# A long convolution on TensorE: reading the moving operand from the loaded kv tile instead of from a built copy

## The chip, the core and the metric

The kernel runs on one NeuronCore of a Trainium2 chip. The time is device microseconds from start to end of one execution; smaller is better. The kernel before takes 864.24 us, the median of three runs (859.52 to 866.49). The profile is of another execution of the same kernel, which took 879.67 us, with a span of 877.8 us from the first to the last instruction.

## The reference

Two independent layers on sequences of S = 2048 with D = 640 channels, all in bf16. Their outputs lie side by side.

```python
# A: a gated long convolution (H3)
k_shift = sum over t < 4 of k[s - t] * shift_k[:, t]
kv = k_shift * v
y = causal convolution of kv with ssm_k along the sequence, per channel (2048 taps)
a = q * (y + kv * ssm_D)
# B: full softmax attention, 32 heads of 20
q, k, v = x @ wqkv
b = softmax(q k^T * 20 ** -0.5) v @ wo
out = concatenate([a, b])
```

The convolution is written as an FFT in the reference; the kernel computes it directly, with matmuls. `ssm_D` is added to the first tap.

## The kernel before

**Attention.** Queries come in four chunks of 512, heads in eight groups of four, keys in 16 blocks of 128. A score unit is one head, one key block, one query chunk: 128 x 512 numbers in one PSUM bank. `S_task` (L629) computes two or three units, then `EXP_task` (L671) has ScalarE take the exponential of two or three banks at once and write bf16 probabilities into slots of `P_sb`. There are 2048 units. When ScalarE would be late, a unit goes to VectorE: `chain_start` reads the bank (L691), and for two units together `chain_end` works out the exponential in six steps (L726 to L731, then L721 or L723). `PV_task` (L749) multiplies four probability tiles with V. The rest (projections L473, transposes L447 and L773, output L835) is fitted between.

**Convolution.** A prologue on VectorE (L558) computes kv and stores it in a DRAM scratch, each block of 32 positions reversed. For each channel the stationary operand is a window of the kernel's taps (`HK`, a Toeplitz matrix loaded with overlapping rows), and the moving operand holds the channel's kv values, 16 blocks of time as 16 columns, in two parities. `conv_task` (L964) does 16 channels: per channel eight matmuls (L982), each with 26 to 32 columns, adding into one PSUM bank. 40 tasks, 5120 matmuls. Three VectorE steps fold the bank into `Y`; `A_iter` multiplies by q.

The moving operand is built. `kvr_load` brings 80 channels of kv into `KVr` as [128, 64 steps, 80 channels]: the values of one channel at successive steps lie 80 elements apart. `kvx_build` has GpSimd copy them (L957) into `KVX`, two tiles of 16 channels in turn, so that a channel's columns lie side by side. Each build is two copies of 512 elements. There is one `KVr` tile: after the fifth build it is loaded again.

**Order of work.** It is decided when the program is built. `Prog` keeps an estimated time per engine (`T`), and a main loop puts the next score group on PE when its bank is expected free, else whatever fits the slack: side tasks by due time (`pend`), convolution matmuls one by one (each taken as `CQ` = 0.026 us), `PV_task`, or matmuls on zeros (`fill`, L376) when PE streams too little. `dve_run` orders VectorE by priorities, `pool_run` GpSimd's copies. VectorE steps marked `two` are put off while a GpSimd copy is thought to run (`pbusy`). `want_vec` gives a unit to VectorE if its backlog is below `VQ`. All DMA loads of the convolution go through SyncE's queue, in the planned order. So any change of a cost or a buffer reorders the whole program.

**SBUF.** One region `R` holds, in turn, the prologue's tiles and then the convolution's tiles plus `NPX` extra probability slots. `NPU` slots exist in all.

```python
dst = sub(KVX[i], [[64, 8], [16, 4], [1, 16]], 512 * z)                  # kvx_build: operand, side by side
src = sub(KVr, [[1, 8], [80, 4], [320, 16]], t % 5 * 16 + 8 * z)         # from steps of 320 elements
rhs = sub(KVX[i], [[32, 2], [1, n]], (4 * u + x) * 64 + r1 * 16)         # conv_task: moving operand
```

## Time and profile before

| | busy us, or count |
|---|---|
| span | 877.8 |
| PE matmul (ends modelled) | 849.1 |
| ScalarE | 826.4 |
| VectorE | 772.5 |
| GpSimd | 103.0, of which copies L957 90.8 |
| convolution matmuls L982 | 5120, 178 ns each (modelled, overlapping) |
| zero matmuls L376 | 435 |

Busy times overlap between engines and don't add up to the span. [...]the distance between starts, best seen at the weight loads (PEld), says more about the rate. The mean granted TensorE clock in this execution is 0.949 of full speed.

### The profile page before, as it was taken

Reading aid. Unit: us, or ns where it says so; the run is one execution under the profiler, and the core shown is the slowest. Engines: PE = TensorE matmul, PEld = TensorE weight load, DVE = VectorE, ACT = ScalarE, POOL = GpSimd, SP = SyncE. Lnnn points to the kernel's source line nnn. Section 1 sums busy time; section 2 is a strip of 40 time slices with the busy share of each in tenths; the row PEclk is TensorE's granted clock in tenths of the full one; section 3 lists DMA queues with packets and bytes.
Section 4 is the critical chain, followed back from the end, with each engine's and each line's share of the span. In section 5 each row is a group of like instructions: output and inputs, shape, how many; then the busy total and the mean of one; then the engine's idle time right before and its main releaser. Section 6 shows DMA issues by size and latency. Waiting matters only on the chain.

```text
span 877.8 us, 27035 instructions
## 1 busy us (share of the span) xinstructions
PE 849.1 (97%) x11659; PEld 359.4 (41%) x11659; DVE 772.5 (88%) x1582; ACT 826.4 (94%) x738; POOL 103.0 (12%) x95
## 2 busy tenths in 40 slices
PE   9999999998999999999999999999999999999998
PEld 5432332222345444444344444435444443443432
DVE  4457899998699999999999999999998999986794
ACT  6799999998799999999999999999998999997796
POOL 3000000003021111121112001211120211010000
PEclk9999999999599999999999999999998999985599
DMA  9614422228259887878866867897595789584512
GB/s 282 220 37 141 140 91 91 91 62 140 67 140 185 177 189 164 176 170 184 175 150 164 171 165 186 201 173 170 145 182 113 185 188 187 142 188 110 115 26 59
DMA packets 172994, 130.35 MB, mean 148 GB/s; under 512 B 76977, under 2 KB 170155, under 8 KB 172875
## 3 DMA queue, kind: packets, MB, share of 16 engines
q1 hardware_dynamic: 170683, 125.51, 61.9%
q0 software_dynamic: 736, 2.75, 0.9%
q8 instruction: 92, 1.51, 0.8%
q10 hardware_dynamic: 1456, 0.37, 0.2%
q14 instruction: 27, 0.22, 0.1%
HBM read 120.58 MB, written 10.61 MB: 149 GB/s over the span
## 4 chain that ended last, share of the span: by engine, by line
DVE 34%; PE 34%; ACT 30%; issue 1%; DVEq 0%
ACT R L671 30%; PE PS L629 10%; PE PS L982 7%; DVE XV L691 7%; PE PS L749 5%; PE PS L376 4%; DVE XF L728 4%; DVE XF L731 3%; PE PS L473 3%; DVE R L721 3%; DVE R L558 3%; DVE XF L729 2%; DVE XF L726 2%; DVE XF L727 2%; PE PS L835 1%
## 5 line engine op out<-in xcount | busy, mean ns | idle before, releaser
L671 ACT ACTIVATE R<-PS 128x1024 bf16<-128x1024 f32 (+1 forms) x730 | 821.8, 1353 | 37.8 <-PE PS L629 37.2
L629 PE MATMUL PS<-QT,KT 20*128 20x512 bf16 x2048 | 294.7, 400 | 13.6 <-ACT R L671 5.3
L982 PE MATMUL PS<-R 128*128 128x32 bf16 (+3 forms) x5120 | 216.2, 178 | 0.2
L982 PEld LDWEIGHTS PS<-R 128*128 128x128 bf16 x5120 | 165.5, 97 | 109.4 <-issue 101.4
L691 DVE TENSOR_SCALAR XV<-PS 128x512 uint16<-128x512 f32 x249 | 170.5, 687 | 32.1 <-PE PS L629 30.3
L749 PE MATMUL PS<-R,V_sb 128*21 128x512 bf16 x2048 | 172.4, 400 | 3.2 <-DVE R L721 2.3
L629 PEld LDWEIGHTS PS<-QT,KT 20*128 20x128 bf16 x2048 | 71.4, 91 | 209.2 <-ACT R L671 155.4
L957 POOL COPY R<-R 128x512 bf16<-128x512 bf16 x80 | 90.8, 1135 | 519.0 <-PE PS L982 474.2
L376 PE MATMUL PS<-Zt 128*128 128x512 bf16 x435 | 144.9, 404 | 1.2 <-DVE Zt L370 1.0
L731 DVE TENSOR_TENSOR XF<-XF 128x1024 bf16<-128x1024 bf16 x125 | 88.8, 711 | 0.9
L728 DVE TENSOR_TENSOR XF<-XF 128x1024 bf16<-128x1024 bf16 x125 | 87.6, 704 | 0.4
L749 PEld LDWEIGHTS PS<-R,V_sb 128*21 128x21 bf16 x2048 | 37.5, 90 | 75.1 <-issue 46.2
L558 DVE TENSOR_TENSOR R<-R 128x640 bf16<-128x640 bf16 x128 | 61.2, 487 | 2.5
L721 DVE TENSOR_TENSOR R<-XF,XV 128x1024 uint16<-128x1024 bf16 x81 | 58.2, 719 | 0.8
L473 PE MATMUL PS<-xT,WQ 128*20 128x512 bf16 (+1 forms) x660 | 52.8, 396 | 3.6 <-DVE XV L691 3.6
L729 DVE TENSOR_SCALAR XF<-XF 128x1024 bf16<-128x1024 uint16 x125 | 54.2, 436 | 0.6
L726 DVE TENSOR_SCALAR XF<-XV 128x1024 uint16<-128x1024 uint16 x125 | 53.2, 435 | 0.1
L727 DVE TENSOR_SCALAR XF<-XF 128x1024 bf16<-128x1024 uint16 x125 | 52.5, 427 | 0.3
L376 PEld LDWEIGHTS PS<-Zt 128*128 128x128 bf16 x435 | 35.2, 99 | 38.1 <-issue 28.1
L473 PE MATMUL PS<-xT,R 128*20 128x512 bf16 (+2 forms) x660 | 45.5, 374 | 0.3 <-DVE QT L459 0.2
L723 DVE TENSOR_TENSOR R<-XF,XV 128x512 uint16<-128x512 bf16 x87 | 34.6, 425 | 0.4
L459 DVE CAST KT<-PS 128x512 bf16<-128x512 f32 (+1 forms) x32 | 21.4, 675 | 14.6 <-PE PS L473 14.5
(56 smaller groups left out, 347.9 us busy)
## 6 DMA issues: line engine op xcount, KB each, us to landing
R<-kext_scratch SPq DMA_DIRECT2D x640, 136.0 KB, 3.4
R<-in_A_k_dram SPq DMA_DIRECT2D x15, 640.0 KB, 4.0
kext_scratch<-in_A_ssm_k_dram POOLq DMA_DIRECT2D x1, 2560.0 KB, 11.5
R<-in_A_v_dram SPq DMA_DIRECT2D x16, 160.0 KB, 5.8
kvr_scratch<-R SPq DMA_DIRECT2D x16, 160.0 KB
R<-kvr_scratch SPq DMA_DIRECT2D x8, 320.0 KB, 5.8
R<-in_A_q_dram SPq DMA_DIRECT2D x64, 40.0 KB, 3.1
out_dram<-R SPq DMA_DIRECT2D x64, 40.0 KB, 3.1
```

Of the source, the lines that this page charges most:

```text
L376: P.op("pe", lambda e: e.matmul(bank[bk], Zt, zrhs, start=start, stop=start, skip_group_check=True), reads=[b_Zt], writes=[bkb[bk]], tok=s ...
L473: ins = e.matmul(bank[bk][32 * i:32 * i + DH, 0:n], Wt[:, cc, off + i * DH:off + (i + 1) * DH], xT[:, cc, x0:x0 + n], start=(cc == 0), sto ...
L558: P.op("dve", lambda e: e.tensor_tensor(o, a, b, op), reads=reads, writes=writes, c=0.486, two=True)
L629: ins = e.matmul(bank[b0 + i], KT[32 * u:32 * u + DH, g, kb * 128:(kb + 1) * 128], QT[32 * u:32 * u + DH, qs(qc, g), :], start=True, stop= ...
L671: P.op("act", lambda e: e.activation(P_sb[:, s0:s0 + m, :], PS[:, b0 * 512:(b0 + m) * 512].rearrange("p (u q) -> p u q", u=m), ACT.Exp, sc ...
L691: work(0.2, [(lambda e: e.tensor_scalar(V, bank[bk], scale * 1.4426950408889634 * 128.0, 127.0 * 128.0, op0=ALU.mult, op1=ALU.add), [bkb[b ...
L721: last = [(lambda e: e.tensor_tensor(o, Q2, V2, ALU.add), bv + [bq], [b_P[z] for z in zs], two, True)]
L728: (lambda e: e.tensor_tensor(Q, Q, F.bitcast(U16), ALU.mult), [bf, bq], [bq], two, True),
L731: (lambda e: e.tensor_tensor(Q, Q, F, ALU.mult), [bf, bq], [bq], two, True)] + last, end)
L749: ins = e.matmul(bank[OBANK][32 * u:32 * u + DH + 1, :], V_sb[:, kb, 4 * g + u, :], P_sb[:, slot[4 * b + u], :], start=first, stop=last, t ...
L957: steps.append((lambda e, dst=dst, src=src: e.tensor_copy(dst, src), [cv["KVr"]], [kx], 1.3, False))
L982: P.op("pe", lambda e, o=o, lhsT=lhsT, rhs=rhs, st=st, k=k: e.matmul(o, lhsT, rhs, start=st, stop=k == 7, skip_group_check=True), reads=rd ...
```

## The change

The moving operand is read where the load put it. `KVr` now holds 64 channels, and a channel's successive columns lie 4 x 64 elements, 512 bytes, apart; the matmul's access pattern steps over them. `kvx_build`, `KVX`, `pool_run` and GpSimd's part in the convolution go. There are two `KVr` tiles in turn (ten loads instead of eight), and the next load of a tile goes out when the last of its four convolution tasks is planned. The purpose is to save GpSimd's copies, [...]and a link in the chain from load to matmul. The two larger tiles need room: probability slots go from 35 to 33. Several of the planner's constants change with it.

```diff
-NPU, NPX = 35, 11
+CHW, NKR = 64, 2
+NPU, NPX = 33, 9
-OBS = 99
+OBS = 28
-KBV, KBW, LONE = 13, 12, 16
+KBV, KBW, LONE = 13, 12, 24
-KV0, KVPACE, APACE, VQ, CONVE, ZTH, AGE, WAIT3 = 25.0, 0.8, 0.25, 4.5, 60, 2.3, 32, 0.4
+KV0, KVPACE, APACE, VQ, CONVE, ZTH, AGE, WAIT3 = 20.0, 0.8, 0.25, 4.5, 70, 2.4, 40, 0.4
-ZSL, ZLO = 0.45, 1.8
+ZSL, ZLO = 0.3, 1.8
...
-        KVr = carve(KVR_E).rearrange("p (j c) -> p j c", j=64)
-        KVX = [carve(KVX_E) for _ in range(2)]
+        KVr = [carve(KVR_E).rearrange("p (j c) -> p j c", j=64) for _ in range(NKR)]
...
         def kvr_load(b):
-            P.dmas("sp", [(KVr[32 * a:32 * a + 32, 16 * a:64, :],
-                           ap(kvr_d, [[D, 32], [32 * D, 64 - 16 * a], [1, 80]], 80 * b)) for a in range(4)],
-                   d_kvr, reads=b_kvd, writes=[cv["KVr"]], slow=2)
+            P.dmas("sp", [(KVr[b % NKR][32 * a:32 * a + 32, 16 * a:64, :],
+                           ap(kvr_d, [[D, 32], [32 * D, 64 - 16 * a], [1, CHW]], CHW * b)) for a in range(4)],
+                   d_kvr[b % NKR], reads=b_kvd, writes=[cv["KVr"][b % NKR]], slow=2)
...
-        def kvx_build(t):
-            i = t % 2
-            kx = cv["KVX"][i]
-            steps = []
-            for z in range(2):
-                dst = sub(KVX[i], [[64, 8], [16, 4], [1, 16]], 512 * z)
-                src = sub(KVr, [[1, 8], [80, 4], [320, 16]], t % 5 * 16 + 8 * z)
-                steps.append((lambda e, dst=dst, src=src: e.tensor_copy(dst, src), [cv["KVr"]], [kx], 1.3, False))
-            pworks.append(Work(0, steps, lambda: kvr_load(t // 5 + 1) if t % 5 == 4 and t < 39 else None))
...
-                        rhs = sub(KVX[i], [[32, 2], [1, n]], (4 * u + x) * 64 + r1 * 16)
+                        rhs = sub(KVr[i], [[2 * CHW, 2], [4 * CHW, n]], r1 * CHW + c0 + 4 * u + x)
...
-                            if u == 3 and bt + 2 < 40:
-                                kvx_build(bt + 2)
+                            b = bt * 16 // CHW
+                            if u == 3 and c0 + 16 == CHW and b + NKR < D // CHW:
+                                kvr_load(b + NKR)
```

## The prediction

> **What bounds the kernel now.** I read the page's totals first, then the groups, the waits, the span in stretches of 5 us with the chain beside them, and the timeline around the odd stretches.

> ```profile
> PE 849.1 (97%) x11659; PEld 359.4 (41%) x11659; DVE 772.5 (88%) x1582; ACT 826.4 (94%) x738; POOL 103.0 (12%) x95
> ...
> PEclk9999999999599999999999999999998999985599
> ...
> L671 ACT ACTIVATE R<-PS 128x1024 bf16<-128x1024 f32 (+1 forms) x730 | 821.8, 1353 | 37.8 <-PE PS L629 37.2
> L982 PE MATMUL PS<-R 128*128 128x32 bf16 (+3 forms) x5120 | 216.2, 178 | 0.2
> L957 POOL COPY R<-R 128x512 bf16<-128x512 bf16 x80 | 90.8, 1135 | 519.0 <-PE PS L982 474.2
> ```

> PE's 97% is modelled ends, so I don't take PE for the bound. ScalarE is: one line, the exponential, is busy 821.8 us of a span of 877.8, and loses only 37.2 us to late score matmuls. The waits say the same from the other side:

> ```profile
> PEld PS L629 <- ACT R L671: 155.4, 384, 1.6
> ...
> ACT R L671 <- PE PS L629: 37.2, 59, 4.1
> ```

> The score matmuls wait 155.4 us for ScalarE to hand back PSUM banks. PE also runs 435 matmuls on zeros that compute nothing. So PE has slack on average, and VectorE (88%) has some too.

> Where do the 37.2 us lie? In the stretches of 5 us, columns are PE, PEld, DVE, ACT, POOL busy, then the granted clock:

> ```profile
> 210.00:215.00 5.00, 3.74 (x38) 0.86 (x36) 4.97 (x7) 4.27 (x5) 4.80 (x4) 1.00 0.74 139
> 215.00:220.00 5.00, 3.90 (x28) 0.68 (x27) 3.44 (x7) 2.85 (x4) 0.02 (x1) 0.58 0.00 0
> 220.00:225.00 5.00, 5.00 (x31) 0.75 (x29) 2.60 (x6) 3.44 (x4) 0.00 (x0) 0.50 0.00 0
> ```

> The clock falls to half in three stretches: 215 to 245, about 660 to 667, and 782 to 839 us. ScalarE is busy 21.3 of 30 us in the first, 11.3 of 15 around the second (655 to 670), and 45.4 of 60 around the third: lost are 8.7, 3.7 and 14.6 us, together 27.0. The profiled execution took 879.7 us; without these it would be 852.7. The timed median, 864.2, lies 11.5 above that, near the first two together (12.4). I take it that these two recur and the third mostly doesn't; that is an inference.

> What starts the first is in the timeline:

> ```profile
> 210.01 5.01 POOL L957 COPY R<-R 128x512 bf16<-128x512 bf16 x4 [10.27 <-DMA R<-kvr_scratch]
> 210.37 1.32 DVE L726 TENSOR_SCALAR XF<-XV 128x1024 uint16<-128x1024 uint16 x1
> 211.73 1.22 DVE L727 TENSOR_SCALAR XF<-XF 128x1024 bf16<-128x1024 uint16 x1
> 212.87 0.68 DVE L691 TENSOR_SCALAR XV<-PS 128x512 uint16<-128x512 f32 x1
> 213.69 0.39 PE L629 MATMUL PS<-QT,KT 20*128 20x512 bf16 x3 [1.14 <-DVE XV L691]
> 214.13 2.06 ACT L671 ACTIVATE R<-PS 128x1024 bf16<-128x1024 f32 x2 [0.73 <-PE PS L629]
> ```

> Four operand copies run back to back on GpSimd. Two VectorE steps that take 422 ns at the median take 1320 and 1220. The PSUM read behind them is not slower, but starts late, so its bank comes free late, PE idles 1.14 us, ScalarE 0.73, and half clock follows. At 655.49 two copies (2.78 us) stretch the same kind of step to 1.31 us and PE's next weight loads wait 0.67 and 0.92 us for that same PSUM read; half clock follows there too.

> [...]422 becomes 1320, while the PSUM reader stays at 680. [...]half clock follows PE's idling. [...]34 convolution weight loads take 0.92 us, last one 0.096, so (0.92 - 0.096)/33 = 25.0 ns. [...]

> **The change, part by part.**

> *Copies removed.* 80 copies of 1135 ns, 90.8 us of GpSimd, which is idle otherwise. GpSimd itself is on no path. What they cost VectorE: mean over median times count, over the seven SBUF steps of the vector exponential: 124 x (14 + 7 + 19 + 15 + 27 ns) + 81 x 32 + 87 x 6 = 10.2 + 2.6 + 0.5 = 13.3 us. That is small because the planner puts other work beside a copy, and VectorE has about 105 us idle. On the path it counts where it set off half clock: up to 8.7 + 3.7 us. I credit the first in full, since the four queued copies are the setup of the convolution, and half of the second[...]: -8.7 - 1.8 = -10.5.

> *The plan's new split.* The build shows 260 units on VectorE against 249, and exponentials 412 of 1024 and 321 of 1536 columns with 3 of 512, against 391, 339 and 2. Back to back, two of 1536 take 2.79 us with 1.45 for the last: a step of 1.34; three of 1024 take 2.86 with 1.02: 0.92. So ScalarE gets 21 x 0.92 - 18 x 1.34 + 0.5 = -4.3 us, on the path. VectorE gets 11 units: per pair of units two reads at 0.60, three scalar steps at 0.34 and three tensor steps at 0.60 (starts in its timeline) make 4.0 us, so 2.0 each, 22 us. Hidden: 13.3 regained and 105 idle stand against it.

> *The moving operand.* Each matmul now reads 26 to 32 columns of bf16, each 512 bytes from the last. Lower bound: nothing, if reading stays under the 25 ns. Nearest rows for strided reads: VectorE reads PSUM with 64 bytes between elements at full rate (256 elements 418 ns, 512 contiguous 687: the same slope with one overhead). GpSimd's copy, stepping 640 bytes in SBUF, needs 1097/512 = 2.14 ns an element; 29 columns at that rate are 62 ns, my upper bound. [...]The contiguous rate is 512 columns in about 216 ns (eight V-product matmuls, four at a time, end 0.21 us after four), 0.42 ns each; doubled 0.84, so 32, 30, 28, 26 columns take 26.9, 25.2, 23.5, 21.8 ns. Only the first two exceed 25: 1280 x (1.9 + 0.2) = 2.7 us over all. I take this value. Most hides in PE's wait for ScalarE. To see how much, I summed for each gap between score groups in the new order PE's work at the steps above against 0.45 us of ScalarE per score unit: 44 gaps overrun by 6.5 us at 24.8 ns, 59 by 9.3 at 27.5. A fifth of that difference: +0.5. The same sum gives +7 at 30 ns, +30 at 40, +60 at 50, +106 at 62.

> *Loads.* Ten of 640 KB instead of eight of 800: the same 6.4 MB, but 51,200 rows of 128 bytes for 40,960 of 160. A part lands in 4.6 to 6.8 us; with two tiles a load goes out when its tile's last convolution is done, four tasks ahead of need. Convolution runs from 226 to 842 us in 40 tasks, 15.4 us each, so 60 us of lead hide it. The new wait is the transfer queue's, for that last matmul; behind it stand weight loads that wait for the same matmul already. GpSimd's clearing grows from 3.3 to two of 2.6 us (by elements); only the first holds the first load. Nothing on the path.

> *Fewer probability slots (33 for 35), 446 zero matmuls for 435, other constants.* 11 x 0.216 = 2.4 us of PE in gaps; 17 more stand ahead of the convolution, where the first half-clock stretch was. Counted zero.

> Sum: 864.2 - 10.5 - 4.3 + 0.5 = 849.9, say **850 us**.

> **Rivals.** *Strided reads slow TensorE* (chance 0.16). [...]Against: the 25 ns floor leaves room for a halved rate, and PE waits 155 us for ScalarE. At 40 to 62 ns the overruns give 850 + 30 to 850 + 106: 880 to 956, more if stalled columns also lower the clock. *The gain is eaten* (0.22): half clock comes from thin stretches of small matmuls, as at 782 us, where no stretched VectorE step stands ahead, and the new order has its own; or the step becomes 30 ns (+7); or VectorE's extra 22 us holds banks. Then 864.2 - 4.3 and a few us either way: 856 to 868. The main case has 0.62, 840 to 856: a little above 840 if all 27 us of half clock were gone too, as 852.7 - 4.3 = 848 is the floor of the order of before, less some of the smaller VectorE delays.

> The range, 838 to 872, takes in the first two cases and leaves out most of the slow one. Faster by over 1% means under 855.6, slower over 872.9.

> **What would show it.** No GpSimd copies and no VectorE SBUF step over about 0.8 us; the exponential's busy time near 817 us; no half clock near 215 us; convolution weight loads still 25 to 26 ns apart within a run. Wrong if that distance is 30 ns or more, or if ScalarE's waits for the score matmuls exceed 37 us at full clock.

## The result, and the profile after

The changed kernel takes 1199.6 us against 865.4, medians of four executions each: the ratio is 1.386, 95% interval 1.372 to 1.399. Executions of one kernel differ in how long the clock stays at half (the kernel before took from 850.0 us at a mean clock of 1.000 to 881.6 at 0.944), so the ratios, and the times from the table on, are of executions within 1.5% of the fastest of that kernel on the same occasion. Forecast were 850 us, with a range to 872. The rival "strided reads slow TensorE" had given 880 to 956; the result is beyond that too.

The page of the changed kernel: totals, the granted clock in 40 slices, the exponential (L672 now), convolution weight loads and matmuls (L972), and the zero matmuls.

```profile
PE 1182.2 (99%) x11656; PEld 500.5 (42%) x11670; DVE 790.0 (66%) x1616; ACT 866.3 (72%) x742; POOL 14.4 (1%) x16
...
PEclk9999997565568665577655569555875555655659
...
L672 ACT ACTIVATE R<-PS 128x1024 bf16<-128x1024 f32 (+1 forms) x734 | 861.8, 1253 | 316.7 <-PE PS L630 313.0
...
L972 PEld LDWEIGHTS PS<-R 128*128 128x128 bf16 x5120 | 288.3, 119 | 172.1 <-issue 169.3
L972 PE MATMUL PS<-R 128*128 128x32 bf16 (+3 forms) x5120 | 357.4, 228 | 0.2 <-DVE R L993 0.2
...
L376 PE MATMUL PS<-Zt 128*128 128x512 bf16 x446 | 199.5, 524 | 1.0 <-DVE Zt L370 1.0
```

The zero matmuls of the kernel before:

```profile
L376 PE MATMUL PS<-Zt 128*128 128x512 bf16 x435 | 144.9, 404 | 1.2 <-DVE Zt L370 1.0
```

Three things stand here. ScalarE went from 94% to 72% and now waits 313.0 us for score matmuls, against 37.2: the bound has moved to PE. A convolution matmul takes 228 ns instead of 178. And work that the change doesn't touch is slower: a zero matmul takes 524 ns instead of 404. The clock line says why. From about 195 us to the end the clock is mostly at half; the mean is 0.677 of full speed.

How far apart the convolution matmuls start is read in the timeline, from weight loads that follow each other. First the kernel before, then the changed one in a stretch at full clock (PEld alone):

```profile
300.65 0.92 PEld L982 LDWEIGHTS PS<-R 128*128 128x128 bf16 x34 [0.23 <-issue]
...
306.66 0.94 PEld L972 LDWEIGHTS PS<-R 128*128 128x128 bf16 x18 [0.23 <-issue]
307.70 0.10 PEld L630 LDWEIGHTS PS<-QT,KT 20*128 20x128 bf16 x3
308.02 0.95 PEld L972 LDWEIGHTS PS<-R 128*128 128x128 bf16 x18 [0.23 <-issue]
```

Before it is (0.92 - 0.1)/33 = 25 ns, after (0.95 - 0.1)/17 = 50 ns; the 0.1 us is the last load itself (94 ns at the shortest in the changed kernel). Over all runs of 16 or more such loads the median is 50.5 ns after and 24.7 before, and at half clock it is about the same (from one start to the next after a matmul of 28 columns: 50 ns at full and at half clock in the changed kernel, 25 and 27 before). So two questions stand: what makes the matmul take 26 ns more, and how 5120 x 25.8 ns = 132 us become 335.

### The profile page after: what moved, and what is told of

It is laid out like the page before. It is cut to its first block, busy times and chain, and to the rows that moved or that the text cites. A ratio compares the mean times of both kernels' runs of the same rounds, so it can differ in the third digit from the quotient of the medians.

```text
span 1197.3 us, 26976 instructions
## 1 busy us (share of the span) xinstructions
PE 1182.2 (99%) x11656; PEld 500.5 (42%) x11670; DVE 790.0 (66%) x1616; ACT 866.3 (72%) x742; POOL 14.4 (1%) x16
## 4 chain that ended last, share of the span: by engine, by line
PE 83%; ACT 9%; DVE 7%; issue 1%; DVEq 0%
PE PS L972 25%; PE PS L630 23%; PE PS L750 15%; PE PS L376 12%; ACT R L672 9%; PE PS L473 4%; PE PS L836 2%; DVE R L559 2%; DVE XV L692 1%; PE PS L774 1%; DVE KT L459 1%; PE PS L805 1%; DVE XF L732 0%; PE PS L531 0%; DVE XF L727 0%
## 5 line engine op out<-in xcount | busy, mean ns | idle before, releaser
L672 ACT ACTIVATE R<-PS 128x1024 bf16<-128x1024 f32 (+1 forms) x734 | 861.8, 1253 | 316.7 <-PE PS L630 313.0
L630 PE MATMUL PS<-QT,KT 20*128 20x512 bf16 x2048 | 374.2, 507 | 6.3 <-ACT R L672 1.5
L972 PEld LDWEIGHTS PS<-R 128*128 128x128 bf16 x5120 | 288.3, 119 | 172.1 <-issue 169.3
L972 PE MATMUL PS<-R 128*128 128x32 bf16 (+3 forms) x5120 | 357.4, 228 | 0.2 <-DVE R L993 0.2
L750 PE MATMUL PS<-R,V_sb 128*21 128x512 bf16 x2048 | 230.2, 523 | 2.5 <-DVE OT_sb L760 2.2
L376 PE MATMUL PS<-Zt 128*128 128x512 bf16 x446 | 199.5, 524 | 1.0 <-DVE Zt L370 1.0
L473 PE MATMUL PS<-xT,WQ 128*20 128x512 bf16 (+1 forms) x660 | 64.5, 476 | 0.0
L727 DVE TENSOR_SCALAR XF<-XV 128x1024 uint16<-128x1024 uint16 x130 | 55.5, 435 | 0.0
L990 DVE COPY ZS<-PS 64x256 f32<-64x256 f32 x40 | 16.7, 418 | 33.7 <-PE PS L972 33.3
L760 DVE CAST OT_sb<-PS 128x512 bf16<-128x512 f32 x32 | 22.0, 688 | 25.2 <-PE PS L750 25.0
L459 DVE CAST QT<-PS 128x512 bf16<-128x512 f32 (+1 forms) x32 | 21.7, 679 | 22.9 <-PE PS L473 22.9
## 6 DMA issues: line engine op xcount, KB each, us to landing
kext_scratch<-in_A_ssm_k_dram POOLq DMA_DIRECT2D x1, 2560.0 KB, 11.3
```

What stands on the lines that cost most here:

```text
L376: P.op("pe", lambda e: e.matmul(bank[bk], Zt, zrhs, start=start, stop=start, skip_group_check=True), reads=[b_Zt], writes=[bkb[bk]], tok=s ...
L473: ins = e.matmul(bank[bk][32 * i:32 * i + DH, 0:n], Wt[:, cc, off + i * DH:off + (i + 1) * DH], xT[:, cc, x0:x0 + n], start=(cc == 0), sto ...
L630: ins = e.matmul(bank[b0 + i], KT[32 * u:32 * u + DH, g, kb * 128:(kb + 1) * 128], QT[32 * u:32 * u + DH, qs(qc, g), :], start=True, stop= ...
L672: P.op("act", lambda e: e.activation(P_sb[:, s0:s0 + m, :], PS[:, b0 * 512:(b0 + m) * 512].rearrange("p (u q) -> p u q", u=m), ACT.Exp, sc ...
L727: (lambda e: e.tensor_scalar(F.bitcast(U16), V, 127, None, op0=ALU.bitwise_and), bv, [bf], one, True),
L750: ins = e.matmul(bank[OBANK][32 * u:32 * u + DH + 1, :], V_sb[:, kb, 4 * g + u, :], P_sb[:, slot[4 * b + u], :], start=first, stop=last, t ...
```

## Experiments

In each, "distance" is the median distance of convolution weight loads in runs of 16 or more: (length of the run - 0.1 us)/(count - 1). Half clock is 2 x (1 - mean clock) x span.

| run | moving operand | distance, ns | us | mean clock | half clock, us |
|---|---|---|---|---|---|
| before | built, 2 bytes apart | 24.7 | 864.2 | 0.949 | 90 |
| after | kv tile, 512 bytes apart | 50.5 | 1199.1 | 0.677 | 773 |
| e1 | built, 128 bytes | 51.2 | 1213.4 | 0.659 | 827 |
| e4 | built, 16 bytes | 52.9 | 1227.7 | 0.644 | 878 |
| e3 | built, 8 bytes | 27.9 | 868.3 | 0.970 | 52 |
| e8, e10 | built, 4 bytes | 24.7 | 843.4, 843.8 | 1.000 | 0 |
| e2 | changed plan, 2 bytes | 24.7 | 854.0 | 0.978 | 38 |
| e5 | changed plan, 114 columns side by side | 49.5 | 967.8 | 0.993 | 14 |
| e6 | changed plan, half of the channels 512 bytes | 37.6 | 980.7 | 0.870 | 253 |

Times are medians. Distance, clock and half clock are of the profiled executions, which took 879.7 us for before, 873.9 for e3 and 1235.6 for e4. In the three series of experiments the kernel before ran beside them on the same chip, with medians of 859.5, 860.1 and 859.8 us.

### e1, e4, e3: the step alone

These are the kernel before, with its plan, its copies and its loads. Only the order of elements within `KVX` changes, and with it the step between a channel's columns.

```diff
-dst = sub(KVX[i], [[64, 8], [16, 4], [1, 16]], 512 * z)
+dst = sub(KVX[i], [[1, 8], [16, 4], [64, 16]], 8 * z)      # e1
...
-rhs = sub(KVX[i], [[32, 2], [1, n]], (4 * u + x) * 64 + r1 * 16)
+rhs = sub(KVX[i], [[32, 2], [64, n]], 4 * u + x + r1 * 16)      # e1: 128 bytes
+rhs = sub(KVX[i], [[256, 2], [8, n]], (4 * u + x) // 8 * 512 + (4 * u + x) % 8 + r1 * 128)   # e4: 16 bytes
+rhs = sub(KVX[i], [[128, 2], [4, n]], (4 * u + x) // 4 * 256 + (4 * u + x) % 4 + r1 * 64)    # e3: 8 bytes
```

The last three lines are the three variants. In e4 and e3 the copies write in groups of 8 and 4 channels accordingly (not shown).

Theory L in what follows: once neighbouring columns lie too far apart, each costs TensorE about 1.67 ns, however far. The 1.67 is from the changed kernel, 57 ns after a matmul of 32 columns and 47 after one of 26. The first figures for e3 are for the case that 8 bytes are near enough.

> The kernel before, its plan unchanged, with the built operand laid out so that a channel's columns lie 128 bytes apart. Theory L[...]: convolution weight loads 48 to 50 ns apart as in the changed kernel, long stretches at half clock, and a time of 1130 to 1230 us. Theory B (the step of 512 bytes is the trouble[...]): 25 to 35 ns apart and under 950 us. Theory P (the new plan or the loads are the trouble, not the reading): time as before, 860 to 880 us.

> The same in groups of 8 channels: columns 16 bytes apart[...]. Theory L: as with 128 bytes, 48 to 50 ns and 1130 to 1230 us. If the cost grows with the step: between 25 and 48 ns, and between.

> The kernel before with the built operand in groups of 4 channels: columns 8 bytes apart[...]. [...]weight loads 25 to 27 ns apart and 855 to 880 us. If any step beyond one element costs: over 30 ns, and over 900 us.

Measured: e1 1213.4 us (ratio 1.415, 1.400 to 1.430) and e4 1227.7 (1.432, 1.412 to 1.451). Nothing of the new plan is in them, and the whole loss is. e3 takes 868.3 (862.7 and 873.9; two further executions, with more half clock, took 888.7 and 915.0; ratio 1.013, 0.999 to 1.026), which can't be told from before. Weight loads of e4 and of e3 at full clock, (1.70 - 0.1)/30 = 53 ns and (0.57 - 0.1)/17 = 28 ns:

```profile
330.32 1.70 PEld L982 LDWEIGHTS PS<-R 128*128 128x128 bf16 x31 [0.23 <-issue]
...
312.96 0.57 PEld L982 LDWEIGHTS PS<-R 128*128 128x128 bf16 x18 [0.23 <-issue]
```

Theory P (plan, loads) and theory B (something about 512 bytes) fall. The cost sets in between 8 and 16 bytes and stays the same up to 512: 52.9, 51.2, 50.5 ns. No step between 8 and 16 bytes was run, and what sets the cost in there is not shown. The page of e4 shows the clock under the plan of before:

```profile
PEclk9999999555755555657555555665555555656679
```

In e1 and e4 GpSimd's copies, which now write with a step, also grew, to 2551 and 2568 ns (1418 in e3, 1135 before), and their times hold what that costs. It may be why e4 is some 28 us slower than the changed kernel, which has no copies. The step without copies is in e2.

### e2: the changed plan without the step

```diff
-rhs = sub(KVr[i], [[2 * CHW, 2], [4 * CHW, n]], r1 * CHW + c0 + 4 * u + x)
+rhs = sub(KVr[i], [[2 * CHW, 2], [1, n]], r1 * CHW + c0)
```

> The changed kernel, its plan unchanged, with each matmul reading its columns side by side (the wrong columns of the kv tile: the convolution's numbers are not the reference's). Theories L and B: 25 ns between weight loads, the clock near full, and the time that was predicted for the change without the reading: 845 to 862 us. Theory P: still over 1100 us.

Measured: 854.0 us (853.3 and 854.7; two further executions, with more half clock, took 873.9 and 891.7), before on the same chip 859.5 (850.0 to 861.2): no difference that can be told. So the step alone makes the loss, and the rest of the change gains nothing that can be told from the noise; 850 was predicted for this part. Its profile, of the execution of 854.7 us, has VectorE undisturbed but for one step, and half clock in two places: the clock line, then the first place in stretches of 5 us (PE, PEld, DVE, ACT, POOL busy, the clock, the DMA engines' share and GB/s):

```profile
PEclk9999999999999999999999999999999589799999
...
660.00:665.00 5.00, 4.15 (x41) 1.30 (x37) 4.45 (x10) 5.00 (x5) 0.00 (x0) 0.74 0.52 137
665.00:670.00 5.00, 5.00 (x57) 1.96 (x55) 3.25 (x6) 3.33 (x4) 0.00 (x0) 0.50 0.38 81
```

No copy runs there: the new order has thin stretches of its own, as the rival "the gain is eaten" had it.

### e5, e6: the longer matmul against the slower clock

e5 makes the matmul as long as the strided one, but with data: 114 columns side by side. All go to the same PSUM columns, so the convolution's numbers are lost. e6 reads every second channel at 512 bytes.

```diff
 # e5
-rhs = sub(KVr[i], [[2 * CHW, 2], [4 * CHW, n]], r1 * CHW + c0 + 4 * u + x)
-o = sub(bank[MISC], [[256, 2], [1, n]], (4 * u + x) * 16 + d)
+rhs = sub(KVr[i], [[2 * CHW, 2], [1, 57]], r1 * CHW + c0)
+o = sub(bank[MISC], [[256, 2], [1, 57]])
 # e6
+rhs = sub(KVr[i], [[2 * CHW, 2], [4 * CHW if x % 2 else 1, n]], r1 * CHW + c0 + (4 * u + x) * (x % 2))
```

> The changed kernel, its plan unchanged, each convolution matmul reading 114 columns side by side instead of 26 to 32 at 512 bytes (wrong columns, all added into the same ones: the convolution is left out in effect). The matmul takes as long as the strided one, but the array streams all the while. Theory C (waiting for the operand keeps the array idle, the clock is gated to half, and that is most of the loss): weight loads about 50 ns apart, the clock above 0.95, and 880 to 950 us. Theory D (the 26 ns more per matmul are the loss by themselves): about 1200 us.

> The changed kernel, its plan unchanged, every second channel read at 512 bytes, the others side by side (wrong columns for these). Mean distance about 38 ns, 66 us more of matmul than with none strided. If the loss is in proportion: about 1030 us. [...]with the clock mostly full 880 to 920 us, with it mostly half over 1080 us.

The page of e5:

```profile
PE 951.8 (99%) x11656; PEld 478.2 (49%) x11670; DVE 784.4 (81%) x1616; ACT 844.9 (87%) x742; POOL 14.4 (1%) x16
...
PEclk9999999979999999999999999999999999999999
```

and its matmuls, kept apart by shape:

```profile
L972 PE MATMUL PS<-R 128*128 128x114 bf16 x5120 | 355.1, 215 | 0.2 <-DVE R L993 0.2
...
L376 PE MATMUL PS<-Zt 128*128 128x512 bf16 x446 | 144.4, 391 | 1.0 <-DVE Zt L370 1.0
```

The same order of instructions, the same 50 ns, and 967.8 us instead of 1199.1: the clock stays at 0.993, the zero matmul takes 391 ns. (It is 18 us above the range expected.) So of some 345 us between e2 and the changed kernel, 968 - 854 = 114 come from the longer matmul and 1199 - 968 = 231 from the clock. e6, with 38 ns, is at 980.7 and 0.870. In proportion it would be 854 + 345/2 = 1027. It lies between the two sides that were written down, so it says only that the loss grows faster than the share of strided matmuls.

Over all twelve traces, from 20 us to the last windows, each of the 42 full-clock windows filled under 0.40 was followed by half clock, 40 of the 94 between 0.40 and 0.50, and none above 0.52; no window under 0.74 brought full clock back. So filling under about half puts the clock at risk, and only filling of about three quarters or more brought it back, and that not each time. This is an estimate, worked out from starts and shapes. What the runs show is that the time a strided matmul takes beyond 0.42 ns a column, in which I take its columns to stall, works like idle time, while PE shows 99% busy: e5 and the changed kernel have the same order and the same distance (49.5 and 50.5 ns), and differ in how much of it columns stream and in the clock (0.993 and 0.677).

### e7, e8, e10: what the copies cost

e7 is the kernel before with each copy cut to 16 elements (the convolution reads stale data). e8 and e10, the same kernel, copy pairs of channels as 32-bit elements and leave nothing out.

```diff
 # e8, e10
-dst = sub(KVX[i], [[64, 8], [16, 4], [1, 16]], 512 * z)
-src = sub(KVr, [[1, 8], [80, 4], [320, 16]], t % 5 * 16 + 8 * z)
+dst = sub32(KVX[i], [[64, 4], [16, 4], [1, 16]], 256 * z)      # the tile seen as 32-bit integers
+src = sub32(KVr, [[1, 4], [40, 4], [160, 16]], t % 5 * 8 + 4 * z)
...
-rhs = sub(KVX[i], [[32, 2], [1, n]], (4 * u + x) * 64 + r1 * 16)
+rhs = sub(KVX[i], [[64, 2], [2, n]], (4 * u + x) // 2 * 128 + (4 * u + x) % 2 + r1 * 32)
```

> The kernel before, its plan unchanged, each GpSimd copy cut from 512 elements to 16 (the operand is mostly not built, so the convolution's numbers are not the reference's). If the copies cost what was predicted, by setting off half clock near 215 and 660 us: 8 to 12 us less than before, no half clock at 215 us. If that half clock has another cause: no difference that can be told.

> The kernel before, its plan unchanged, the copies done on pairs of channels as 32-bit elements, half as many, so that a channel's columns lie 4 bytes apart; the result is the reference's. Theory L: weight loads 24.7 to 26 ns apart. If GpSimd's time goes by elements, copies take 0.6 us instead of 1.1, and the time is 0 to 6 us below before.

> The kernel before with copies of pairs of channels as 32-bit elements once more, for an interval. If its gain is that copies of half the length no longer set off half clock: 840 to 850 us in most runs, 1.5 to 2.5% below before. If it was the chip of the day: no difference.

Measured: e7 843.6 us (ratio 0.980, 0.975 to 0.984), e8 843.4 (0.979, 0.971 to 0.986), e10 843.8, six executions from 842.9 to 844.9 (0.980, 0.975 to 0.985). One more execution of e8 took 871.0 us at a mean clock of 0.953, so pair copies don't rule half clock out. The copies did cost, some 17 us, more than the 10.5 that I credited and than I expected of e7 (8 to 12) and e8 (0 to 6), and halving them wins all of it. One execution of the kernel before, beside e1 to e4, kept full clock throughout and took 850.0 us: by that one, some 10 of the 17 us are the half clock and some 6 are not. e10 beats both kernels. Its timeline at the place where half clock began before:

```profile
210.45 2.97 POOL L962 COPY R<-R 128x256 int32<-128x256 int32 x4 [10.02 <-DMA R<-kvr_scratch]
...
211.29 0.86 DVE L731 TENSOR_SCALAR XF<-XV 128x1024 uint16<-128x1024 uint16 x1
...
212.19 0.74 DVE L732 TENSOR_SCALAR XF<-XF 128x1024 bf16<-128x1024 uint16 x1
...
213.67 0.39 PE L634 MATMUL PS<-QT,KT 20*128 20x512 bf16 x3 [0.46 <-DVE XV L696]
```

The four copies take 2.97 us instead of 5.01, the VectorE steps 0.86 and 0.74 instead of 1.32 and 1.22, PE idles 0.46 instead of 1.14, and the clock stays full to the end:

```profile
PE 820.4 (97%) x11659; PEld 355.9 (42%) x11659; DVE 758.3 (90%) x1582; ACT 820.3 (97%) x738; POOL 65.1 (8%) x95
...
PEclk9999999999999999999999999999999999999999
```

With a step of 4 bytes the distance is 24.7 ns, as side by side.

### e9: the planner told the truth

```diff
-CQ = 0.026
+CQ = 0.049
```

> The changed kernel with the planner told 0.049 us for a convolution matmul instead of 0.026; the reading stays at 512 bytes. The build then leaves 2304 of the 5120 convolution matmuls for after the last score group and puts in 996 zero matmuls instead of 446. Theory C: while attention runs, short runs of strided matmuls between zeros keep the clock mostly full, and the 2304 left at 50 ns add some 115 us: 960 to 1040 us, below the changed kernel. If strided reading gates the clock however it is mixed: still about 1200 us or more.

Two executions took 1193.1 and 1299.1 us; the profile is of the second. The expectation of theory C, 960 to 1040 us, failed: the faster one too is level with the changed kernel. In stretches of 100 us (columns as above):

```profile
900.00:1000.00 100.00, 100.00 (x772) 34.20 (x770) 67.58 (x138) 72.35 (x61) 0.00 (x0) 0.52 0.35 74
1000.00:1100.00 100.00, 99.29 (x1077) 61.97 (x1075) 19.83 (x47) 23.45 (x18) 0.00 (x0) 0.87 0.62 145
1100.00:1200.00 100.00, 99.39 (x1148) 70.30 (x1146) 11.99 (x37) 0.00 (x0) 0.00 (x0) 1.00 0.88 185
```

In this execution attention lasts to about 1030 us, much of it at half clock, and the convolution left over runs some 245 us after it, with 552 of the 996 zeros in between, which I had not counted. That leaves 444 zeros for the time of attention, as many as the changed kernel has in all (446), so the run doesn't test whether more zeros there would keep the clock full. After attention the clock is full (1.00 in the last stretch) with strided matmuls among zeros: strided reading does not lower it in every mixture. By the count above that fits: 552 zeros of 0.22 us and some 2300 convolution matmuls of 12 ns fill about 0.6 of the 245 us. There the distance rises to about 60 ns; why is open. What e9 shows is that this way of planning around the slow matmul doesn't mend it.

## Why the prediction was wrong

**The moving operand** is the step that failed, in two terms.

The first is its rate. I took 0.84 ns a column, by doubling the 0.42 ns of columns side by side; the doubling was my own estimate, shown by no run. At that rate 29 columns take 24 ns and stay under the 25 ns between starts. Measured are 50.5/29 = 1.74 ns at 512 bytes, twice my value, and the same at full and at half clock. The number of columns shows it too: in the changed kernel the next convolution matmul starts 47 ns (median) after one of 26 columns and 57 after one of 32, (57 - 47)/6 = 1.67 ns for each further column. At 8 bytes it is 27.9/29 = 0.96; at 4 and 2 bytes the 24.7 ns between starts hide it; in the kernel before a start comes 25 ns after one of 26 columns and after one of 32. So a column 16 bytes or more from the last costs 1.7 to 1.8 ns (52.9/29 = 1.82 at 16), and one 8 bytes from it 0.96 at most. From 8 bytes to 16 the distance does about double (27.9 to 52.9), but what doubles is not 0.42 ns a column. I had the upper bound, 2.14 ns from GpSimd's copy, on the page, and gave it 0.16; it was the only measured row of a strided SBUF read, and close to the truth.

The second term is what the longer matmul does to the rest. My sum over gaps gave +60 us at 50 ns. With the clock nearly full it is 114 (e5 against e2): the waits that I counted on hid less of it. The other 231 us I had left as "more if stalled columns also lower the clock". The sign was before me: three drops to half clock in the profile of before, each after a thinly filled stretch, and two of them tied to idle PE. I used them to credit the change with fewer drops, and didn't ask what the strided reads themselves do to filling.

**Copies removed**: right in mechanism, too small in size. -10.5 was credited, all of it for half clock; e7 gives some -17 with the plan unchanged. Half clock is about what was credited, by the one execution of before at full clock (850.0 us). The other 6 us or so are not broken down; I had counted the stretched VectorE steps beside the copies as hidden.

**The plan's new split** (-4.3) can't be seen: e2 has it and the copies' removal, worth some 17 us by e7, and yet can't be told from before. So the new order gives back most of that; how much of it by its own half clock (38 us in e2) is not separated. VectorE's steps are undisturbed as foretold, but for one: the two clearings of the kv tiles, which I costed at nothing. The timeline of the changed kernel:

```profile
192.25 5.53 POOL L934 MEMSET R<- 128x3072 bf16 x2 [154.88 <-DMA kvr_scratch<-R]
...
192.80 2.38 DVE L727 TENSOR_SCALAR XF<-XV 128x1024 uint16<-128x1024 uint16 x1
...
195.82 0.78 PE L750 MATMUL PS<-R,V_sb 128*21 128x512 bf16 x8 [1.70 <-DVE OT_sb L760]
```

Beside them a VectorE step takes 2.38 us instead of 0.42 (median), as beside the copies (1.32), PE idles 1.70 us, and the first half clock of the changed kernel begins here. A step stretched alike (2.33 us) in e2 isn't followed by half clock, so it is not shown that the clearings alone bring it.

**Loads**: right. No convolution matmul of the changed kernel waits for a kv load.

**Busy time near 817 us** for the exponential: 814.2 in e2; 861.8 in the changed kernel, where instructions stand apart and overlap less: 734 of 1253 ns make 920 us, of which 58 overlap, against 730 of 1353 ns, 988 us, of which 166 did before.

## What to carry to other kernels

A matmul's moving operand wants its neighbouring columns close together: 8 bytes apart cost 27.9 ns a matmul here, 16 bytes 52.9. If a copy is needed for that, pairs of bf16 channels moved as 32-bit elements (columns 4 bytes apart) gave the full rate at about 0.6 of the copy's time. When an engine's price for an access is unknown and one measured row shows a similar access, put real weight on that row. And where the profile shows the TensorE clock falling, ask of every change how it alters the share of time in which columns stream, since PE, stalled for its operand, looked 99% busy here and yet lost the clock.

## What the runs showed that I had not expected

The clock's share of the loss (231 of 345 us) was larger than the matmuls' own. The clock fell at fillings under about half but returned only at about 0.75 or more, so one thin window can cost many: 54.6 us at once in the kernel before. And making a kernel stream more useless columns, 114 instead of 29 in e5, made it 231 us faster than the same order with stalled ones.
